# Key differences for both key halves of the first head group, with new planner settings

## The chip, the cores and the metric

The kernel runs on one core of one Trainium2 chip. The metric is device time in microseconds of one execution; a kernel's time is the median over its runs.

## The reference

Two transformer layers over 2048 rows of 512 columns. Each layer is an attention block with 32 heads of 16 columns and a gated feed-forward block of 1792 columns, both on a layer norm and both added back to x.

```python
def attention(x, wqkv, wo):            # x: (1, 2048, 512)
    q, k, v = split(x @ wqkv)          # 32 heads of 16 columns
    scores = einsum("bhqd,bhkd->bhqk", q, k) * 16 ** -0.5
    return merge(einsum("bhqk,bhkd->bhqd", softmax(scores), v)) @ wo

def ffn(x, w_gate, w_up, w_down):      # w_gate, w_up: (512, 1792)
    return (gelu(x @ w_gate) * (x @ w_up)) @ w_down

for layer in range(2):                 # the same weights in both
    x = x + attention(layernorm(x), A_wqkv, A_wo)
    x = x + ffn(layernorm(x), B_w_gate, B_w_up, B_w_down)
```

## The kernel before

**Units and tiles.** Heads go in groups of four (`NG` = 8), because four heads of 16 columns fit TensorE's four row groups of 32. The queries of a layer are cut into blocks (four of 512 in the first layer, three of 512 and two of 256 in the second, the last two handled in halves near the end). A unit `u` is one query block of one head group. A score tile is 128 queries of one head by 512 keys (one key block, `kb` 0 to 3); there are 4096 score tiles in all.

**Two passes over the scores.** The softmax needs a row maximum. In the first pass ("p1") TensorE makes a score tile with queries on the partitions (L1628) and VectorE reduces it to its row maximum in `PM` (L1643), one or two tiles per instruction. When a unit's maxima are all there, `fin_step` (L981 to L1012) joins the four key blocks' maxima in six small GpSimd operations, and a DVE transpose and four small DMAs (L1007, L1023) write the negated maximum into spare rows of the queries `QT`. In the second pass ("p2") TensorE makes the scores again, transposed, with the maximum already subtracted (L1510), ScalarE takes the exponential into `PT` (a view of `SCR`; L1487, one or two tiles per instruction), and TensorE multiplies by the values and a column of ones (L1533) into bank 7. `nrm` (L1031) divides.

**Folds.** VectorE has more to do in the first pass than ScalarE in the second at some times, so a pair of score tiles can be "folded". For key blocks a and b of one half of the keys, max(qa, qb) = qb + relu(qa - qb). GpSimd makes the key difference `KD` = KT[a] - KT[b] of the group once (`kd`, L1231 to L1243, the subtraction at L1240). TensorE multiplies the queries by it (L1460), ScalarE takes the Relu into `PT` (L1467), GpSimd writes a very negative maximum in place of tile a (L1470), and one custom VectorE instruction adds the Relu to tile b in PSUM and takes the maximum (L1638). Two VectorE tile reductions become one pass, and ScalarE gets one more. `f_list` holds the tiles that may be folded, in p1 order; `f_head` (L1404) drops those that p1 has passed, and `want_fold` (L1418) decides whether a fold is wanted. There are `NKD` = 2 buffers for differences. Before the change each unit has one pair of key blocks for its folds, and its buffer is `u % NKD`:

```python
pair = {u: (2, 3) if u == 0 else (0, 1) for u in range(NU)}
f_list = [h for h in p1_list if h[2] == pair[h[0]][0]]
```

**The order of the work.** The program is not looped on the chip. A planner at build time (the loop at L1668) steps through a model of the five engines and writes out each engine's instructions in order. It works through `p1_list`, keeps the second pass behind the first by a lag, and puts everything else (projections, layer norms, output projection, feed-forward pieces, differences) as chains with due times between them. For the first unit `p1_list` takes key block 0 of all queries first and key blocks 1 to 3 after that (L692). Every 32 score tiles (`STRETCH` = 16 pairs) the planner reads a new row of `PLAN`, 129 rows of 19 settings: how long an engine may wait for a joint start (`SPC`, `SPLIT`), lags from which evacuations change engine (`LAGT`) or the second pass gets more banks (`LAG`), whether pairs of banks may go to one exponential at two places (`P2B`), margins for folds (`FL`, `FX`), the size of projection pieces (`PIECE`, `GP`) and so on. PSUM evacuations go to VectorE (L766 `tensor_copy`) or ScalarE (L768) by `pick`. The same holds for the residual additions (L1064 on VectorE, L1069 with L1071 on ScalarE and GpSimd) and the gate products (L1195, or L1201 with L1203). Where TensorE would idle, the planner puts fill products on zeros (L1661).

In the head of the program GpSimd also clears the key buffers `KT` (the copies at L558), makes layer-norm scales (L581 to L585), normalises some rows (L592, which may also go to VectorE or ScalarE) and copies rows of x (L1293).

Of the kernel before, what the change touches and what calls it, by code (L numbers as in the profile page):

```python
# [310 lines left out]
def _build(nc, x_in, wqkv, wo, wg, wu, wd, out, layer_blocks=((512, 512, 512, 512), (512, 512, 512, 256, 256)),  # L311
# [16 lines left out]
    with es:  # L328
# [902 lines left out]
        def kd(u):  # L1231
# [4 lines left out]
            if pos["g"] >= f_end[u]:  # L1236
                return
# [653 lines left out]
```

## Time and profile before

| | |
|---|---|
| median of three runs | 2494.56 us (2493.24 to 2499.01) |
| the profiled execution's own time | 2493.29 us |
| its span | 2491.6 us |
| VectorE busy | 2417.7 us, 97% |
| ScalarE busy | 2339.2 us, 94% |
| TensorE busy | 2380.4 us, 96% |
| GpSimd busy | 1309.8 us, 53% |
| reductions at L1643 | 2595 instructions, mean 926 ns |
| exponentials at L1487 | 2484 instructions, mean 910 ns |
| folds at L1638 | 160 instructions, mean 686 ns |
| differences at L1240 | 74 instructions, mean 1153 ns |

The span runs from the first to the last instruction. Busy time is the union of an engine's instructions; neighbours on one engine may overlap a little in the records, so a mean duration is somewhat longer than the distance from one start to the next. In a group's line the number after the bar is busy time, then the mean of one, then the engine's idle time just before them with what ended it.

### The profile page before, as it was taken

What the parts mean: (1) busy time and instruction counts of PE and PEld (TensorE: products, weight loads), DVE (VectorE), ACT (ScalarE), POOL (GpSimd) and SP (SyncE); (2) the same over time, 40 slices, a digit from 0 to 9 for tenths busy, and PEclk for the clock granted to TensorE, in tenths of its full rate; (3) what the DMA queues carried; (4) which work ended last, traced back from release to release, by engine and by line L of the source; (5) the groups of instructions that cost most, each with busy time, mean ns of one, the idle gap of its engine ahead of it and who ended that gap; (6) DMA issues with size and microseconds to landing.
All of it is one profiled execution on the core that took longest, in us unless ns stands there. A gap on an engine that the chain in (4) does not pass through costs nothing.

```text
span 2491.6 us, 68681 instructions
## 1 busy us (share of the span) xinstructions
PE 2380.4 (96%) x29395; PEld 1138.3 (46%) x29648; DVE 2417.7 (97%) x3198; ACT 2339.2 (94%) x3189; POOL 1309.8 (53%) x2158
## 2 busy tenths in 40 slices
PE   7999999999999999999999999999999999999999
PEld 2444444444444444444433555554444444554456
DVE  9999999999999999999999999999999999999994
ACT  6999999999999999999965999999999999999996
POOL 5121138856788356877242211278617882269462
PEclk9999999999999999999999999999999999999999
DMA  3110000000000000000000000000000000000000
GB/s 94 48 57 6 6 2 9 2 4 4 4 4 2 2 7 4 4 10 2 17 7 12 5 4 4 4 4 2 2 13 6 2 3 11 4 3 4 9 5 10
DMA packets 27354, 25.09 MB, mean 10 GB/s; under 512 B 9513, under 2 KB 26025, under 8 KB 27049
## 3 DMA queue, kind: packets, MB, share of 16 engines
q1 hardware_dynamic: 27048, 20.69, 2.9%
q8 instruction: 232, 3.80, 0.6%
q14 instruction: 74, 0.60, 0.1%
HBM read 9.70 MB, written 2.10 MB: 5 GB/s over the span
## 4 chain that ended last, share of the span: by engine, by line
DVE 40%; PE 37%; ACT 22%; issue 1%; POOL 0%; DMA 0%; SPq 0%; ACTq 0%; POOLq 0%; DVEq 0%
DVE PM L1643 38%; ACT SCR L1487 20%; PE PS L1628 12%; PE PS L751 9%; PE PS L1533 8%; PE PS L1510 3%; PE PS L1661 3%; DVE SCR L1638 1%; ACT SCR L1127 1%; ACT SCR L1467 0%; PE PS L873 0%; PE PS L1460 0%; DVE HT L592 0%; ACT HT L768 0%; ACT AO L1201 0%
## 5 line engine op out<-in xcount | busy, mean ns | idle before, releaser
L1643 DVE TENSOR_REDUCE PM<-PS 128x1 f32<-128x512 f32 (+1 forms) x2595 | 2235.5, 926 | 30.8 <-PE PS L1510 9.3
L1487 ACT ACTIVATE SCR<-PS 128x1024 bf16<-128x1024 f32 (+1 forms) x2484 | 2029.4, 910 | 68.7 <-PE PS L1510 46.8
L1628 PE MATMUL PS<-KT,QT 32*128 32x512 bf16 x3936 | 1046.3, 384 | 54.4 <-DVE PM L1643 32.7
L1510 PE MATMUL PS<-QT,KT 32*128 32x512 bf16 (+2 forms) x4736 | 945.6, 354 | 6.0 <-ACT SCR L1487 5.0
L1533 PE MATMUL PS<-VP,SCR 128*128 128x51 bf16 (+1 forms) x16384 | 810.7, 187 | 11.8 <-ACT SCR L1487 6.8
L1533 PEld LDWEIGHTS PS<-VP,SCR 128*128 128x128 bf16 x16384 | 573.3, 96 | 497.6 <-issue 420.9
L1628 PEld LDWEIGHTS PS<-KT,QT 32*128 32x128 bf16 x3936 | 249.3, 91 | 533.3 <-DVE PM L1643 329.1
L1661 PE MATMUL PS<-WV,ZER 128*128 128x240 bf16 x1948 | 365.9, 266 | 4.8 <-ACT SCR L1487 3.4
L1051 POOL TENSOR_TENSOR RL<-ACCS,CM 128x16 f32<-128x16 f32 (+2 forms) x66 | 179.4, 2718 | 340.4 <-ACT ACCS L1045 340.0
L1510 PEld LDWEIGHTS PS<-QT,KT 32*128 32x128 bf16 x4736 | 239.0, 91 | 65.2 <-ACT SCR L1487 40.0
L996 POOL TENSOR_TENSOR PM<-PM 128x32 f32<-128x32 f32 (+2 forms) x74 | 18.0, 243 | 327.6 <-DVE PM L1643 320.8
L1661 PEld LDWEIGHTS PS<-WV,ZER 128*128 128x128 bf16 x1948 | 148.0, 96 | 61.0 <-issue 48.2
L1203 POOL TENSOR_TENSOR HT<-HT,AO 128x512 bf16<-128x512 bf16 x98 | 113.6, 1161 | 103.6 <-ACT AO L1201 103.1
L1240 POOL TENSOR_TENSOR KD<-KT 128x512 bf16<-128x512 bf16 x74 | 85.3, 1153 | 92.9 <-PE PS L1460 61.0
L751 PE MATMUL PS<-XNT,WU 128*128 128x512 bf16 (+2 forms) x498 | 123.6, 333 | 3.8 <-issue 2.5
L751 PE MATMUL PS<-XNT,WG 128*128 128x512 bf16 (+2 forms) x501 | 121.8, 333 | 5.2 <-issue 3.8
L751 PE MATMUL PS<-WD,HT 128*128 128x512 bf16 x384 | 121.2, 381 | 3.1 <-issue 1.3
L1131 POOL TENSOR_TENSOR HT<-HT,SCR 128x512 bf16<-128x512 bf16 (+1 forms) x98 | 106.1, 1083 | 4.7
L1125 POOL TENSOR_TENSOR SCR<-SCR,HT 128x512 bf16<-128x512 bf16 (+1 forms) x98 | 106.0, 1083 | 1.7
L1121 POOL TENSOR_TENSOR SCR<-HT 128x512 bf16<-128x512 bf16 (+1 forms) x98 | 95.8, 978 | 18.2 <-ACT HT L768 12.9
L1638 DVE CUSTOM_DVE_ANT_0 SCR<-PS,SCR 128x512 bf16<-128x512 f32 x160 | 102.8, 686 | 2.6 <-PE PS L1628 0.8
L1071 POOL TENSOR_TENSOR X<-X,AO 128x512 f32<-128x512 f32 x39 | 49.4, 1266 | 101.6 <-ACT AO L1069 101.2
(126 smaller groups left out, 1541.3 us busy)
## 6 DMA issues: line engine op xcount, KB each, us to landing
KT<-SG SPq DMA_DIRECT2D x64, 64.0 KB
QT<-SG SPq DMA_DIRECT2D x56, 64.0 KB
QT<-MT SPq DMA_DIRECT2D x224, 1.0 KB
out_dram<-AO SPq DMA_DIRECT2D x16, 128.0 KB, 1.7
WG<-in_B_w_gate_dram SPq DMA_DIRECT2D x4, 448.0 KB, 4.0
WU<-in_B_w_up_dram SPq DMA_DIRECT2D x4, 448.0 KB, 4.9
WD<-in_B_w_down_dram SPq DMA_DIRECT2D x4, 384.0 KB, 4.8
HT<-in_A_x_dram SPq DMA_DIRECT2D x2, 512.0 KB, 9.0
```

What stands on the lines that cost most here:

```text
L751: ins = e.matmul(out_ap, lhsT=l, rhs=r_, start=(i == 0), stop=(i == n - 1))
L1051: emit("pool", lambda e: e.tensor_tensor(RL[:, s, 0:4 * nq], lsum, CM1[:, 0:4 * nq], op=ALU.pow), r=[("ACCS", s), ("CM1",)], w=[("RL", s)] ...
L1125: emit("pool", lambda e: e.tensor_tensor(u, u, ht, op=ALU.mult), r=[ku, kh], w=[ku], dur=0.18 + n / 520.0)
L1131: emit("pool", lambda e: e.tensor_tensor(ht, ht, u, op=ALU.mult), r=[ku, kh], w=[kh], dur=0.18 + n / 520.0)
L1203: emit("pool", lambda e, ft=ft, o=o: e.tensor_tensor(HV[:, ft, :], HV[:, ft, :], AO[:, o, 0:n], op=ALU.mult), r=[("AO", o)] + ht_keys(ft, ...
L1487: emit("act", lambda e: e.activation(dst, src, ACTF.Exp, scale=DH ** -0.5), r=[BK[bk + i] for i in range(cnt)], w=[("PT", i) for i in slot ...
L1510: ins = e.matmul(bank(bk)[:, i * n:(i + 1) * n], lhsT=KT[32 * j:32 * j + 32, g, kt * 128:(kt + 1) * 128], rhs=QT[32 * j:32 * j + 32, s, 0: ...
L1533: ins = e.matmul(acc, lhsT=PT[:, slot, i * n + qt * 128:i * n + (qt + 1) * 128], rhs=AP(VP, (kt * H + 4 * g + j) * 17, [[NTT * H * 17, 128 ...
L1628: ins = e.matmul(bank(b), lhsT=QT[32 * j:32 * j + 32, s, qt * 128:(qt + 1) * 128], rhs=KT[32 * j:32 * j + 32, g, kb * 512:(kb + 1) * 512], ...
L1638: emit("dve", lambda e, i=i, b=b, sl=sl: e.tensor_tensor_reduce(PT[:, sl, :], bank(b), PT[:, sl, :], 1.0, -3.0e38, ALU.add, ALU.max, po[:, ...
L1643: emit("dve", lambda e: e.tensor_reduce(po, PS[:, bs[0]:bs[0] + cnt, :], axis=AX.X, op=ALU.max), r=bks, w=[("PM", sm) + h[1:] for h in hs] ...
L1661: return e.matmul(PS[:, b, NACC:512], lhsT=ZER[:, :], rhs=WV[:, 0, 0:512 - NACC], start=(b != 7), stop=(b != 7), skip_group_check=True)
```

## The change

`folds` replaces `pair`: a unit may fold in key half 0 (blocks 0 and 1), and units below `DP` = 1, so the first one alone, in half 1 (blocks 2 and 3) as well. Differences, their records and buffers are kept for a unit and a half instead of a unit: `f_seq` numbers them in p1 order, and the buffer is that number modulo `NKD`. In `fin_step` the maxima of neighbouring key blocks are now compared by stride instead of by first and second half, for all units, so that in each comparison the block whose maximum a fold replaces comes first. And 94 of the 129 rows of `PLAN` have new numbers: rows 0 to 5, 18 to 65, 73 to 79, and nearly all from 90 on.

```diff
 PLAN = [
-    (0.1, 0.0, 0.65, 0.42, 0.3, -0.05, 1, 1, 62, 84, 8, 80, 0.3, 2.0, 0, 2, 2, 2, 7),
+    (0.1, 0.0, 0.45, 0.12, 0.3, -0.05, 1, 1, 62, 84, 8, 60, 0.3, 1.5, 0, 2, 2, 2, 7),
...
-        pair = {u: (2, 3) if u == 0 else (0, 1) for u in range(NU)}
+        folds = {u: (0, 1) if u < DP else (0,) for u in range(NU)}
         p1_at = {h: i for i, h in enumerate(p1_list)}
-        f_list = [h for h in p1_list if h[2] == pair[h[0]][0]]
+        f_list = [h for h in p1_list if h[2] % 2 == 0 and h[2] // 2 in folds[h[0]]]
         f_end = {}
+        f_gs = []
+        half_p1 = {}
         for h in f_list:
-            f_end[h[0]] = max(f_end.get(h[0], -1), p1_at[h])
+            gi = (h[0], h[2] // 2)
+            if gi not in f_end:
+                f_gs.append(gi)
+                half_p1[gi] = p1_at[h] / 2.0
+            f_end[gi] = max(f_end.get(gi, -1), p1_at[h])
+        f_seq = {gi: i for i, gi in enumerate(f_gs)}
...
             if f["stage"] == 0:
-                lo, hi = pm[:, :, 0:8], pm[:, :, 8:16]
-                if pair[u][0] == 2:
-                    lo, hi = hi, lo
-                a0, a1 = lo[:, :, 0:4], lo[:, :, 4:8]
+                pv = pm.rearrange("p a (h l j) -> p a h l j", h=2, l=2)
+                lo, hi = pv[:, :, :, 0, :], pv[:, :, :, 1, :]
+                a0, a1 = lo[:, :, 0, :], lo[:, :, 1, :]
...
-        def kd(u):
+        def kd(gi):
+            u, hf = gi
             la, bi, t0, n, g = units[u]
-            ka, kb = pair[u]
+            ka, kb = 2 * hf, 2 * hf + 1
+            q = f_seq[gi]
             yield ("cond", lambda: (kt_rec.get((g, ka)) == la and kt_rec.get((g, kb)) == la
-                                    and (u < NKD or pos["g"] > f_end[u - NKD])))
+                                    and (q < NKD or pos["g"] > f_end[f_gs[q - NKD]])))
-            if pos["g"] >= f_end[u]:
+            if pos["g"] >= f_end[gi]:
                 return
-            s = u % NKD
+            s = q % NKD
...
-            for u in range(NU):
-                add(kd(u), first_p1[u] - FDUE)
+            for gi in sorted(f_gs):
+                add(kd(gi), (half_p1[gi] if gi[1] and gi[0] else first_p1[gi[0]]) - FDUE)
```

`f_head`, `f_opts` and `f_emit` look up the unit and half in the same way.

More of the change, by code (lines that the diff above doesn't have):

```diff
@@ L311, in _build @@
 def _build(nc, x_in, wqkv, wo, wg, wu, wd, out, layer_blocks=((512, 512, 512, 512), (512, 512, 512, 256, 256)),
-           n_ahead=6, n_pre=6, S1C=0.45, S2C=0.42, OV=0.3, PD=80, FDUE=20, LIM=-0.05, NT=1, AHD=2.0, DUEM=2, FDL2=0, OPD=12, URG=0.3, ft_tok=512, n_pt=8, n_qt=8, SPLIT=0.15, SPC=0.1, PVC=47, WARM=0.55, WARML=0.42, NPV=7, BOOST=0.0, LAG=62, LAGT=84, GP=2, SING=0, DUE=0, END=360, LAGE=10, FD=205, FDL=-10, QD=60, KD_=16, VD=20, FL=8, FMAX=6, NKD=2, FLOOK=2, FX=0.3, GF=0, FAST=1, TG=1, GS=2, P2B=1, PIECE=2, GL=60, GLE=20, HARD=-1e9, LNP=1, LNPT=12, PREO=1, SPL=2, OPL=1, BM=1, LAGB=60, PREO0=1, LNPT0=8, LNPT1=8):
+           n_ahead=6, n_pre=6, S1C=0.45, S2C=0.42, OV=0.3, PD=80, FDUE=20, LIM=-0.05, NT=1, AHD=2.0, DUEM=2, FDL2=0, OPD=12, URG=0.3, ft_tok=512, n_pt=8, n_qt=8, SPLIT=0.15, SPC=0.1, PVC=47, WARM=0.55, WARML=0.42, NPV=7, BOOST=0.0, LAG=62, LAGT=84, GP=2, SING=0, DUE=0, END=360, LAGE=10, FD=205, FDL=-10, QD=60, KD_=16, VD=20, FL=8, FMAX=6, NKD=2, FLOOK=2, FX=0.3, GF=0, FAST=1, TG=1, GS=2, P2B=1, PIECE=2, GL=60, GLE=20, HARD=-1e9, LNP=1, LNPT=12, PREO=1, SPL=2, OPL=1, BM=1, LAGB=60, PREO0=1, LNPT0=8, LNPT1=8, DP=1):
     S = x_in.shape[1]
@@ L1242, in kd @@
                  r=[("KT", g, ka), ("KT", g, kb)], w=[("KD", s)], dur=1.2)
-            kd_rec.add(u)
+            kd_rec.add(gi)
         hstat = {1}
@@ L1410, in f_head @@
             u = i[0]
-            if u not in kd_rec or u not in qt1_rec or (u >= n_ahead and u - n_ahead not in qp2_rec):
+            if (u, i[2] // 2) not in kd_rec or u not in qt1_rec or (u >= n_ahead and u - n_ahead not in qp2_rec):
                 return None
@@ L1431, in f_opts @@
             h = f_list[0]
+            kdk = ("KD", f_seq[(h[0], h[2] // 2)] % NKD)
             if gel["on"] is not None or h[3] % 2 or f_list[1:2] != [h[:3] + (h[3] + 1,)]:
@@ L1435, in f_opts @@
                     return []
-                tq = max(est([("QT", h[0] % n_qt), ("KD", h[0] % NKD)]), est(w=[("PT", so)]), now)
+                tq = max(est([("QT", h[0] % n_qt), kdk]), est(w=[("PT", so)]), now)
                 bs = (4,) if gel["on"] is not None else (6, 5) if wide else (6,)
@@ L1441, in f_opts @@
                 return []
-            tq = max(est([("QT", h[0] % n_qt), ("KD", h[0] % NKD)]), est(w=[("PT", sp), ("PT", sp + 1)]), now)
+            tq = max(est([("QT", h[0] % n_qt), kdk]), est(w=[("PT", sp), ("PT", sp + 1)]), now)
             return sorted((max(tq, est(w=[BK[b], BK[b + 1]])), b, 2, True) for b in ((3, 5) if wide else (4, 5))
@@ L1451, in f_emit @@
             s = u % n_qt
-            sd = u % NKD
+            sd = f_seq[(u, ka // 2)] % NKD
             sm = u % n_ahead
-            kb = pair[u][1]
+            kb = ka + 1
             def fn(e):
@@ L1567, in p1_turn @@
             for h in rest:
-                if h[2] == pair[h[0]][0]:
-                    f_end[h[0]] = p1_at[h]
+                if h[2] % 2 == 0 and h[2] // 2 in folds[h[0]]:
+                    f_end[(h[0], h[2] // 2)] = p1_at[h]
         def p1_skip():
```

182 rows, old and new, of the table PLAN are left out of this document.

## The prediction

> **What bounds the kernel now.** I read the page first: the busy shares, the row of slices and the chain that ended last.
>
> ```profile
> PE 2380.4 (96%) x29395; PEld 1138.3 (46%) x29648; DVE 2417.7 (97%) x3198; ACT 2339.2 (94%) x3189; POOL 1309.8 (53%) x2158
> ...
> DVE  9999999999999999999999999999999999999994
> ...
> DVE 40%; PE 37%; ACT 22%; issue 1%; POOL 0%; DMA 0%; SPq 0%; ACTq 0%; POOLq 0%; DVEq 0%
> ...
> DVE PM L1643 38%; ACT SCR L1487 20%; PE PS L1628 12%; PE PS L751 9%; PE PS L1533 8%; PE PS L1510 3%; PE PS L1661 3%; DVE SCR L1638 1%; ACT SCR L1127 1%; ACT SCR L1467 0%; PE PS L873 0%; PE PS L1460 0%; DVE HT L592 0%; ACT HT L768 0%; ACT AO L1201 0%
> ```
>
> VectorE (DVE) is busy 97% of the span and full in every slice but the last; its score reductions at L1643 alone are 38% of the chain, the exponentials of ScalarE (ACT) at L1487 are 20%. So the span is the DVE's work, plus its idle time, plus what is left when the last score has been reduced. When that is, the DVE's timeline says:
>
> ```profile
> 2436.50 2.41 DVE L1643 TENSOR_REDUCE PM<-PS 128x1 f32<-128x512 f32 x3
> ```
>
> The last reduction ends at 2436.50 + 2.41 = 2438.9 us. I then cut the span at places that are the same number of score tiles (128 queries by 512 keys; 4096 in all) done in both kernels. The columns are the length, then busy time and count of PE, weight loads, DVE, ACT and POOL.
>
> ```profile
> core 0: us, PE busy (x) PEld busy (x) DVE busy (x) ACT busy (x) POOL busy (x), PEclk, DMA share, GB/s
> 0.00:367.20 367.20, 344.74 (x4051) 162.75 (x4069) 360.57 (x543) 339.40 (x418) 96.79 (x181) 1.00 0.12 36
> 367.20:1192.60 825.40, 784.52 (x9696) 367.95 (x9798) 819.46 (x974) 803.76 (x1145) 584.12 (x964) 1.00 0.02 4
> 1192.60:1729.40 536.80, 523.92 (x6099) 244.20 (x6132) 520.39 (x749) 483.37 (x578) 203.93 (x353) 1.00 0.03 7
> 1729.40:2184.60 455.20, 433.63 (x5450) 206.09 (x5508) 453.09 (x563) 438.57 (x594) 244.56 (x357) 1.00 0.02 6
> 2184.60:2438.90 254.30, 245.14 (x3364) 123.66 (x3397) 246.86 (x323) 239.65 (x392) 172.39 (x288) 1.00 0.02 5
> 2438.90:2468.30 29.40, 28.37 (x477) 17.47 (x479) 6.82 (x17) 26.37 (x37) 7.44 (x17) 1.00 0.04 11
> 2468.30:2491.60 23.30, 20.08 (x269) 16.23 (x272) 10.48 (x39) 8.05 (x31) 0.55 (x1) 1.00 0.04 13
> ```
>
> DVE idle time, length less busy, is 6.6, 5.9, 16.4, 2.1 and 7.4 us in the first five rows, together 38.4. In the sixth (29.4 us) the DVE has next to nothing to do and ACT finishes its exponentials, in the seventh (23.3 us) the last feed-forward block runs. Thus 2438.9 + 29.4 + 23.3 = 2491.6 us of span. The profiled execution took 2493.29 us, 1.69 outside the span; the median of the three runs is 2494.56, 1.27 above it. I work out a difference and apply it to the median.
>
> **What the built order shows of the change.** The change makes key differences for keys 0 to 1023 and 1024 to 2047 of the first head group; a difference allows a "fold" (one DVE pass in place of two tile reductions, with a Relu on ACT). In the changed program's order the first group has 12 folds in its second half, as before, and none in its first half: scores of block 0 are scheduled before block 1's keys exist. The new difference is made and never used. So the named part is one POOL instruction, and the rest of the change is the order that the new settings give. Settings differ for score tiles 0-191, 576-2111, 2336-2559 and from 2880 on; from 2112 to 2880 both orders do the same work for each 128 tiles within 0.2 us. Counts over the whole program, before to after: DVE pair reductions 1181 to 1189, single ones 1414 to 1410, folds 160 to 154; ACT exponentials of 1024 columns 1612 to 1532, of 512 872 to 1032; fill products on PE 1948 to 1925; DMA issues 540 and 540. Nothing of the arithmetic goes away.
>
> **DVE work up to the last reduction.** The groups by shape:
>
> ```profile
> L1643 DVE TENSOR_REDUCE PM<-PS 128x2 f32<-128x1024 f32 x1181 | 1430.4, 1218 | 20.4 <-PE PS L1510 6.5 <-PE PS L1628 5.7
> ...
> L1643 DVE TENSOR_REDUCE PM<-PS 128x1 f32<-128x512 f32 x1414 | 946.2, 681 | 10.4 <-PE PS L1628 3.1 <-PE PS L1510 2.7 <-PE PS L1460 0.3
> ...
> L1638 DVE CUSTOM_DVE_ANT_0 SCR<-PS,SCR 128x512 bf16<-128x512 f32 x160 | 102.8, 686 | 2.6 <-PE PS L1628 0.8 <-PE PS L1460 0.6 <-PE PS L1510 0.2
> ...
> L1064 DVE TENSOR_TENSOR X<-PS,X 128x512 f32<-128x512 f32 x9 | 6.2, 684 | 2.8 <-PE PS L751 2.6
> ...
> L592 DVE TENSOR_SCALAR HT<-HT 128x512 bf16<-128x512 bf16 x8 | 3.9, 551 | 0.0
> ...
> L766 DVE CAST HT<-PS 128x256 bf16<-128x256 f32 x2 | 0.8, 415 | 0.0
> ...
> L766 DVE COPY XNT<-PS 128x512 bf16<-128x512 bf16 x11 | 4.5, 413 | 1.5 <-PE PS L873 1.5
> ```
>
> Two merged rows of the chain give the pace behind these durations:
>
> ```profile
> 558.72 37.17 DVE PM L1643 x44
> ...
> 1601.29 29.56 ACT SCR L1487 x32
> ```
>
> 44 reductions in 37.17 us are 0.845 each, where the mean by the two forms is 0.925: neighbours overlap by 0.08. So a pair costs 1.14, a single 0.60, a fold 0.61. Eight pairs more are +9.1, four singles less -2.4, six folds less -3.7: +3.0. The copies that the planner gives to the DVE instead of ACT: one more of L766 at 256 columns into HT and one into SG (0.33 each), two at 128 into SG (an estimate of 0.2 each from the step between the 256 and 512 forms), two more transposed tiles (0.33 each): +1.7. Two additions of L1064 fewer (0.60 each) and one normalisation of L592 fewer (0.41): -1.6. The 256-column products of L1195 fall from 14 to 10, but up to the last reduction they are 9 and 9. Sum **+3.1 us**, bounds +2 (if the copies are covered by idle time) and +4.
>
> ACT takes two copies of L1069 and four of L1201 more, hands about as many others to the DVE, and gets the split exponentials:
>
> ```profile
> L1487 ACT ACTIVATE SCR<-PS 128x1024 bf16<-128x1024 f32 x1612 | 1583.7, 1070 | 60.2 <-PE PS L1510 43.1 <-PE PS L1628 0.4
> ...
> L1487 ACT ACTIVATE SCR<-PS 128x512 bf16<-128x512 f32 x872 | 522.7, 615 | 8.5 <-PE PS L1510 3.7
> ```
>
> By the means a pair split in two costs 2 x 0.615 - 1.070 = 0.16 us; by the chain row, 32 exponentials in 29.56 us or 0.92 each, the overlap of 0.15 makes it about 0.01. Eighty splits are 0.8 to 12.8 us; the row of neighbours in a run is nearer, so I take about 1. It lies beside DVE work: ACT idles (709.5 - 678.21) = 31.3 us between 1729.4 and 2438.9, as the second row here shows.
>
> ```profile
> 1400.00:1729.40 329.40, 321.92 (x4435) 165.14 (x4452) 321.27 (x420) 328.68 (x376) 135.81 (x219) 1.00 0.02 4
> 1729.40:2438.90 709.50, 678.76 (x8812) 329.76 (x8903) 699.95 (x884) 678.21 (x985) 416.95 (x644) 1.00 0.02 6
> ```
>
> If that cover were gone, the first row shows the price: with ACT full (0.7 us idle of 329.4) the DVE idles 8.1 us, 2.5%.
>
> **The head.** POOL is the engine that gets the added difference (1.15 us), and its fills of KT move: one now stands before the last row block's layer-norm scales, and the DVE's normalisations come as three and four with five and seven tiles around them. How the two engines meet is seen in the first 50 us, DVE rows, then POOL rows:
>
> ```profile
> 8.54 3.97 DVE L592 TENSOR_SCALAR HT<-SCR,HT 128x512 bf16<-128x512 bf16 x2 [0.35 <-POOL HT L603]
> ...
> 24.80 1.37 DVE L592 TENSOR_SCALAR HT<-HT 128x512 bf16<-128x512 bf16 x4
> ...
> 27.83 2.54 DVE L592 TENSOR_SCALAR HT<-HT 128x512 bf16<-128x512 bf16 x4
> ...
> 30.29 15.99 DVE L1643 TENSOR_REDUCE PM<-PS 128x1 f32<-128x512 f32 x19
> ```
>
> ```profile
> 8.58 3.78 POOL L558 COPY KT<-HT 128x2048 bf16<-128x2048 bf16 x2
> ...
> 26.49 1.89 POOL L558 COPY KT<-HT 128x2048 bf16<-128x2048 bf16 x1
> ...
> 28.95 2.45 POOL L1293 CAST X<-HT 128x512 f32<-128x512 bf16 x4
> ...
> 36.15 1.15 POOL L1240 TENSOR_TENSOR KD<-KT 128x512 bf16<-128x512 bf16 x1 [2.91 <-DMA KT<-SG]
> ```
>
> Two DVE normalisations last 3.97 us while POOL's two copies run from 8.58 to 12.36; four others take 1.37 in one place and 2.54 in the other, where POOL's copy of 1.89 (26.49 to 28.38) overlaps their start. The added difference itself follows the one at 36.15, beside reductions (19 in 15.99 us, the 0.84 pace): reductions read PSUM and are not held, so it costs 0 there; what it moves back on POOL is the next group's difference, first needed some 30 tiles later, and the KT fill behind that. The buffers, now given out by halves, add a wait as well: the second group's difference takes the first half's buffer, so it waits until score tile 16; nothing on the DVE waits for it before the folds of the second group. In the new order both groups of normalisations may meet a copy: 0 to 3.8 us against 1.2 now, that is -1.2 to +2.6. PE also has longer stretches without a score tile there (five of over 1.2 us in the first 640 tiles, two before), which can starve the DVE by some tenths each. I take **+1.5**, range -1.2 to +4, since the DVE idle time of the first row (6.6 us) shows that this part is not padded.
> The Trainium skill, page "SBUF — State Buffer", section "SBUF: two separate sides", says that VectorE in a two-port mode and GpSimd share one port pair as an exclusive lock held for a whole instruction, so that the loser blocks fully. By that rule the head could lose the full overlap of both groups, 2.6 us rather than my 1.5; the 3.97 us row agrees with the rule, and the sum would move by 1.1.
>
> **Idle time of the DVE in the changed stretches.** It has 5.9 us in the second row and 9.5 in the fourth and fifth. It comes where PE has long work between two score tiles. These stretches can be counted in both orders, at the paces of the chain in which PE ends last:
>
> ```profile
> 2450.03 1.02 PE PS L751 x4
> ...
> 2451.06 0.34 PE PS L1510 x8
> ```
>
> With 0.25 us for a 512-column product at most, 0.04 for a value product (eight in about 0.31) and a quarter of a pass for row-group tiles, stretches of over 1.0 us from tile 2944 on are 16 before and 10 after; from 640 to 2048 they are five and six. So 9.5 us might fall to 9.5 x 10/16 = 5.9 (-3.6), or not at all. I take **-1.5**, nearer to nothing, as the many shorter waits stay.
>
> **The tail.** Between the last score tile and the last exponential the new order has 46 exponential tiles where there were 54, 4 gate products of 256 columns for 18, and 411 matmuls for 492. That stretch is a chain of PE and ACT:
>
> ```profile
> by line: PE PS L1510 27.9%; PE PS L751 25.7%; PE PS L1533 20.1%; ACT SCR L1487 15.4%; ACT L1148 4.0%; PE PS L1661 2.9%; issue 1.5%; ACT HT L1182 1.0%; ACT SCR L1127 0.9%; ACT SQ L1148 0.6%; ACT ACCS L1045 0.4%
> ```
>
> In proportion to matmuls 29.4 x 411/492 = 24.6: **-4.8 us**. Bounds: four pairs at 0.92 are -3.7; with 14 gate products at 0.13 more, -5.5. After the last exponential both programs have the same 288 matmuls, and 23.3 us stay. The DVE has done more by then, which is the +3.1 above.
>
> **Other moves.** The six POOL steps per group that end the maxima read another layout of the same 32 numbers, and two additions and four products more go to POOL, 53% busy: nothing, under a backlog of about a hundred tiles. No DMA moves in number.
>
> **Sum.** +3.1 + 1.5 - 1.5 - 4.8 = -1.7 us; 2494.56 - 1.7 gives 2492.9, taken as **2493**. That is within 0.2% (5 us, 2489.6 to 2499.5), about what a measurement of this kernel can tell from no change: its three runs alone spread over 5.8 us.
>
> **Rivals.** *The new order removes waits.* The DVE's idle time in the changed stretches halves, (5.9 + 9.5)/2 = 7.7, and the head costs nothing: 3.1 - 7.7 - 4.8 = -9.4, 2485. For it: fewer long PE stretches late, and no added work to speak of. Against: the idle time is already under 1.5% and lies in many short waits; 36%.
> *ACT becomes the bound after the middle.* The 512-column exponentials cluster from tile 2944 on (381 before, 522 after). If splitting costs the 0.16 of the separate means, 70 net splits are 11 us, and with the waits of PE for banks ACT's 31.3 us of idle time go; from then the DVE idles at 2.5% as between 1400 and 1729.4, 709.5 x 0.025 = 17.7 for 9.5: +8.2. Then 3.1 + 1.5 + 8.2 - 4.8 = +8.0, 2502.6. It decides once ACT's idle time there is under some 5 us. Against it: the pace of 0.92. 25%.
> *The change is inert,* the shorter tail and longer reduction part just cancelling, 2494 to 2495: within the forecast's 39%.
>
> The range reaches from near the first rival to the second, 2484 to 2502. Chances: faster 0.36, same 0.39, slower 0.25.
>
> **What would show it.** In the profile after: 154 custom DVE passes; the last reduction at about 2438.9 + 3.1 + 1.5 - 1.5 = 2442; 24 to 26 us from there to the last exponential and 23 after it. Wrong is the head if the DVE's idle time by tile 640 differs by over 4 us from 6.6; wrong is the work term if the DVE's busy time leaves 2417.7 by more than 4; the first rival shows as less DVE idle time in both changed stretches, the second as ACT idle under 5 us late.

## The result, and the profile after

The kernel after takes 2496.58 us (median, 2496.41 to 2501.1), the kernel before 2493.23 in the same comparison (13 runs of each): a ratio of 1.0014, 95% interval 1.0007 to 1.0020, or +3.35 us. The forecast was -1.6. The profiled execution has a span of 2494.6 us, 3.0 longer than before. From its page, the busy line, the DVE's slices and the two rows of the chain that ended last:

```profile
PE 2387.8 (96%) x29366; PEld 1143.7 (46%) x29625; DVE 2421.0 (97%) x3189; ACT 2337.4 (94%) x3267; POOL 1316.8 (53%) x2164
...
DVE  9999999999999999999999999999999999999994
...
PE 44%; DVE 37%; ACT 17%; issue 1%; POOL 0%; POOLq 0%; DVEq 0%; ACTq 0%
DVE PM L1652 35%; ACT SCR L1496 16%; PE PS L1637 15%; PE PS L1542 10%; PE PS L758 10%; PE PS L1519 4%; PE PS L1670 3%; DVE SCR L1647 0%; PE PS L1469 0%; ACT SCR L1476 0%; DVE HT L575 0%; ACT SCR L1133 0%; PE PS L880 0%; DVE HT L592 0%; ACT HT L775 0%
```

Most lines of the program have moved down by five to nine: the reduction is L1652 (was L1643), the exponential L1496 (L1487), the first-pass score tile L1637 (L1628), the second-pass one L1519 (L1510), the value product L1542 (L1533). The DVE still sets the pace, but PE's share of the chain has grown from 37% to 44%, and that of the DVE and ACT has fallen; first-pass score tiles alone are 15% of it, for 12%. The DVE's last reduction, and then the stretches cut at the same numbers of score tiles as in the prediction (length, then busy time and count of PE, weight loads, DVE, ACT, POOL):

```profile
2441.10 5.50 DVE L1652 TENSOR_REDUCE PM<-PS 128x2 f32<-128x1024 f32 x6
```

```profile
core 0: us, PE busy (x) PEld busy (x) DVE busy (x) ACT busy (x) POOL busy (x), PEclk, DMA share, GB/s
0.00:369.00 369.00, 345.77 (x4061) 164.07 (x4078) 361.86 (x541) 339.12 (x417) 98.92 (x186) 1.00 0.12 36
369.00:1194.60 825.60, 789.39 (x9638) 368.83 (x9741) 818.43 (x980) 797.86 (x1153) 583.94 (x963) 1.00 0.02 5
1194.60:1733.00 538.40, 525.54 (x6151) 246.91 (x6182) 520.60 (x748) 485.90 (x581) 206.27 (x355) 1.00 0.03 6
1733.00:2197.30 464.30, 444.24 (x5576) 213.17 (x5642) 461.01 (x556) 449.35 (x682) 249.14 (x362) 1.00 0.02 6
2197.30:2446.60 249.30, 238.93 (x3292) 119.92 (x3319) 243.39 (x317) 235.15 (x379) 173.12 (x287) 1.00 0.02 5
2446.60:2471.30 24.70, 23.84 (x395) 14.54 (x400) 5.17 (x13) 21.95 (x30) 4.84 (x13) 1.00 0.04 13
2471.30:2494.60 23.30, 20.08 (x269) 16.22 (x272) 10.52 (x39) 8.09 (x32) 0.55 (x1) 1.00 0.04 13
```

The last reduction ends at 2446.6, 7.7 us later than before; from there to the last exponential there are 24.7 us in place of 29.4, and 23.3 after it as before. So +7.7 - 4.7 = +3.0. The 7.7 divide by the first five rows into DVE busy time, 2405.3 against 2400.4 (+4.9), and DVE idle time, 7.1, 7.2, 17.8, 3.3 and 5.9 us against 6.6, 5.9, 16.4, 2.1 and 7.4: 41.3 against 38.5, +2.8 (38.4 in the prediction is the sum of rounded terms). (The fourth stretch is longer and the fifth shorter because after runs some 20 second-pass tiles further ahead there.) The groups by shape, DVE and ACT:

```profile
L1652 DVE TENSOR_REDUCE PM<-PS 128x2 f32<-128x1024 f32 x1189 | 1439.5, 1217 | 22.3 <-PE PS L1637 7.4 <-PE PS L1519 6.4
L1652 DVE TENSOR_REDUCE PM<-PS 128x1 f32<-128x512 f32 x1410 | 943.3, 681 | 10.5 <-PE PS L1637 3.2 <-PE PS L1519 3.1 <-PE PS L1469 0.2
L1647 DVE CUSTOM_DVE_ANT_0 SCR<-PS,SCR 128x512 bf16<-128x512 f32 x154 | 99.1, 685 | 2.6 <-PE PS L1637 1.0 <-PE PS L1469 0.6
```

```profile
L1496 ACT ACTIVATE SCR<-PS 128x1024 bf16<-128x1024 f32 x1532 | 1501.4, 1073 | 58.4 <-PE PS L1519 42.7 <-DVE PM L1652 0.5 <-PE PS L1637 0.4
L1496 ACT ACTIVATE SCR<-PS 128x512 bf16<-128x512 f32 x1032 | 604.2, 619 | 15.0 <-PE PS L1519 9.1
```

The counts are those that the prediction read from the order. The head, DVE rows and then POOL rows:

```profile
25.29 2.29 DVE L592 TENSOR_SCALAR HT<-HT 128x512 bf16<-128x512 bf16 x3
...
31.56 2.48 DVE L592 TENSOR_SCALAR HT<-HT 128x512 bf16<-128x512 bf16 x4
```

```profile
24.90 1.89 POOL L558 COPY KT<-HT 128x2048 bf16<-128x2048 bf16 x1
...
30.45 1.89 POOL L558 COPY KT<-HT 128x2048 bf16<-128x2048 bf16 x1
32.28 1.28 POOL L1301 CAST X<-HT 128x512 f32<-128x512 bf16 x2
```

Both groups of normalisations now start under a running copy, where before one of them did.

### The profile page after: what moved, and what is told of

Same layout as the page of the kernel before. It is cut to its first block, busy times and chain, and to the rows that moved or that the text cites. A ratio compares the mean times of both kernels' runs of the same rounds, so it can differ in the third digit from the quotient of the medians.

```text
span 2494.6 us, 68685 instructions
## 1 busy us (share of the span) xinstructions
PE 2387.8 (96%) x29366; PEld 1143.7 (46%) x29625; DVE 2421.0 (97%) x3189; ACT 2337.4 (94%) x3267; POOL 1316.8 (53%) x2164
## 4 chain that ended last, share of the span: by engine, by line
PE 44%; DVE 37%; ACT 17%; issue 1%; POOL 0%; POOLq 0%; DVEq 0%; ACTq 0%
DVE PM L1652 35%; ACT SCR L1496 16%; PE PS L1637 15%; PE PS L1542 10%; PE PS L758 10%; PE PS L1519 4%; PE PS L1670 3%; DVE SCR L1647 0%; PE PS L1469 0%; ACT SCR L1476 0%; DVE HT L575 0%; ACT SCR L1133 0%; PE PS L880 0%; DVE HT L592 0%; ACT HT L775 0%
## 5 line engine op out<-in xcount | busy, mean ns | idle before, releaser
L1652 DVE TENSOR_REDUCE PM<-PS 128x1 f32<-128x512 f32 (+1 forms) x2599 | 2242.8, 926 | 32.9 <-PE PS L1637 10.6
L1496 ACT ACTIVATE SCR<-PS 128x1024 bf16<-128x1024 f32 (+1 forms) x2564 | 2031.8, 890 | 73.4 <-PE PS L1519 51.8
L1637 PE MATMUL PS<-KT,QT 32*128 32x512 bf16 x3942 | 1047.4, 385 | 56.3 <-DVE PM L1652 32.3
L1519 PE MATMUL PS<-QT,KT 32*128 32x512 bf16 (+2 forms) x4736 | 960.0, 354 | 4.4 <-ACT SCR L1496 2.7
L1542 PE MATMUL PS<-VP,SCR 128*128 128x51 bf16 (+1 forms) x16384 | 822.9, 187 | 11.0 <-ACT SCR L1496 6.3
L1542 PEld LDWEIGHTS PS<-VP,SCR 128*128 128x128 bf16 x16384 | 578.3, 96 | 513.6 <-issue 435.0
L1637 PEld LDWEIGHTS PS<-KT,QT 32*128 32x128 bf16 x3942 | 250.0, 91 | 520.6 <-DVE PM L1652 303.8
L1519 PEld LDWEIGHTS PS<-QT,KT 32*128 32x128 bf16 x4736 | 242.6, 91 | 66.9 <-ACT SCR L1496 40.5
L1209 POOL TENSOR_TENSOR HT<-HT,AO 128x512 bf16<-128x512 bf16 (+1 forms) x102 | 116.3, 1142 | 113.6 <-ACT AO L1207 112.2
L1476 ACT ACTIVATE SCR<-PS 128x1024 bf16<-128x1024 f32 (+1 forms) x79 | 81.3, 1029 | 20.6 <-PE PS L1469 18.8
```

The costliest lines, as they stand in the source:

```text
L1209: emit("pool", lambda e, ft=ft, o=o: e.tensor_tensor(HV[:, ft, :], HV[:, ft, :], AO[:, o, 0:n], op=ALU.mult), r=[("AO", o)] + ht_keys(ft, ...
L1496: emit("act", lambda e: e.activation(dst, src, ACTF.Exp, scale=DH ** -0.5), r=[BK[bk + i] for i in range(cnt)], w=[("PT", i) for i in slot ...
L1519: ins = e.matmul(bank(bk)[:, i * n:(i + 1) * n], lhsT=KT[32 * j:32 * j + 32, g, kt * 128:(kt + 1) * 128], rhs=QT[32 * j:32 * j + 32, s, 0: ...
L1542: ins = e.matmul(acc, lhsT=PT[:, slot, i * n + qt * 128:i * n + (qt + 1) * 128], rhs=AP(VP, (kt * H + 4 * g + j) * 17, [[NTT * H * 17, 128 ...
L1637: ins = e.matmul(bank(b), lhsT=QT[32 * j:32 * j + 32, s, qt * 128:(qt + 1) * 128], rhs=KT[32 * j:32 * j + 32, g, kb * 512:(kb + 1) * 512], ...
L1652: emit("dve", lambda e: e.tensor_reduce(po, PS[:, bs[0]:bs[0] + cnt, :], axis=AX.X, op=ALU.max), r=bks, w=[("PM", sm) + h[1:] for h in hs] ...
```

## The experiments

Every time below is a median, compared with the kernel before on the same chip (2493.05 to 2493.22 us in the four comparisons); differences are to that. The 95% intervals of the ratio are up to 0.0013 (3 us) wide to each side. By them the two kernels with tiles moved ahead, the one with groups parted, the code alone, the whole groups moved ahead and after without its new difference are slower than before, and before with all three edits is faster; all other runs can't be told from before by their interval alone. Differences of some tenths of a us rest on the medians.

**Code and settings apart.** The first kernel is before with after's `PLAN`. Its order on PE, DVE, ACT and the DMA queues is after's; it lacks the new difference and keeps the old layout of the maxima. The second is after with before's `PLAN`.

```diff
 # first: the kernel before
-PLAN = [...before's 129 rows...]
+PLAN = [...after's 129 rows...]
```

> The kernel before with the new settings alone (no differences by halves, old layout of the maxima). Its order on TensorE, VectorE, ScalarE and the DMA queue is instruction by instruction that of the changed kernel; GpSimd has one difference less in the head and the old layout of the six maximum steps. Theory A (the settings carry the loss): as slow as the changed kernel, +2.5 to +3.4 us over before, and not more than 1 us faster than the changed kernel. Rival B (the halves of the differences cost it, through GpSimd): within 0.5 us of the kernel before.

2496.23 us, +3.04: the settings carry the loss, and the code on top of them 0.3.

> The changed code with the old settings. Theory A: the added difference has an order of its own only in the first units, so 0 to +2 us over before. Rival B: about +3 us. Rival C (the difference disturbs the order, and the new settings were needed to mend that): clearly worse than both kernels, +5 us or more, with the loss before score tile 512, where its order leaves that of the kernel before; behind tile 640 it is the order of before.

2504.82 us, +11.6 (ratio 1.0039, 1.0027 to 1.0051). The difference shifts the built order, and with the old settings the shifted order is a bad one. Its trace shows where most of it goes: 8.0 us of DVE idle time between score tiles 384 and 512, where before has 0.7. DVE rows, then a PE row:

```profile
240.21 0.69 DVE L773 CAST SG<-PS 128x512 bf16<-128x512 f32 x1 [3.39 <-PE PS L758]
241.71 0.69 DVE L773 CAST SG<-PS 128x512 bf16<-128x512 f32 x1 [0.81 <-PE PS L758]
243.44 1.82 DVE L1652 TENSOR_REDUCE PM<-PS 128x2 f32<-128x1024 f32 x2 [1.04 <-PE PS L1637]
```

```profile
239.14 1.68 PE L758 MATMUL PS<-XNT,WK 128*128 128x512 bf16 x7
```

The key projection of the next head group is late, no score tile can be made, and the DVE waits 3.39 + 0.81 + 1.04 us. So the new settings take up what the added difference does to the order, and bring it back to 3 us behind before. Whether other settings would do so better was not run.

**Which settings.** Three kernels are before with some of after's rows: 90 and up, 18 to 65, 0 to 5 (score tiles 0 to 191, not 0 to 95 as the third expectation has it). Rows 73 to 79 were not run alone.

> The kernel before with the new settings from row 90 (score tile 2880) on alone. By the traces of the two kernels this part loses 7.7 - 2.4 = 5.3 us up to the last reduction and wins 4.7 us behind it: theory A: +0.6 us over before, with the last reduction 5 us later and 24 to 25 us from there to the last exponential. Rival (parts of the order do not add up, the late loss depends on what came before): outside 0 to +1.5 us.

> The kernel before with the new settings in rows 18 to 65 (score tiles 576 to 2111) alone. By the two traces the changed kernel is 1.8 us late at tile 640 and 2.5 us at tile 2176, so theory A gives +0.7 us over before, all of it as VectorE idle time (6 to 7.2 us between tiles 640 and 2048). Rival (parts do not add up): outside 0 to +1.5 us.

> The kernel before with the new settings of score tiles 0 to 95 alone (the first six lines of the list). Theory A (the head loses a part of its own: the DVE's normalisations held by two KT copies on POOL, 1.2 us more than before, and 0.6 us more idle time by tile 128): +1.1 to +1.8 us on the kernel before, 2494.3 to 2495.0, with the normalisations again as two groups of over 2.2 us. By the sum of parts, 3.35 - 0.35 - 1.08 - 0.82 = 1.1 is what is left for these lines. Rival B (the loss hangs on all lines together): 0 within 0.3 us, 2493.2, or over 3 us.

2494.01 (+0.82), 2494.27 (+1.08) and 2494.73 us (+1.61). With the 0.3 of the code they add up to 3.8 for 3.35 measured: no single stretch is at fault, and about half is the head's. The +0.82 of the late rows is a net: the last reduction ends at 2444.1 us, 5.2 later than before, and what follows it is 4.7 shorter. In the head run the normalisations are held as in after:

```profile
25.34 2.28 DVE L592 TENSOR_SCALAR HT<-HT 128x512 bf16<-128x512 bf16 x3
...
31.60 2.47 DVE L592 TENSOR_SCALAR HT<-HT 128x512 bf16<-128x512 bf16 x4
```

**The hold in the head.** From here on kernels keep their instructions and change the order of a few. The recorded operations are laid out again with the moved ones in their new place, and all waits are worked out anew from what each reads and writes.

```diff
+EARLY = [((30, 38), 15)]     # (note) POOL's operations 30 and 38, two KT copies, go behind its operation 15
...
+        sch = sch.again(AHEAD, EARLY)
         sch.plan()
```

> The kernel after with the two KT copies that stood at 24.90 and 30.45 us on POOL moved ahead to where the first two copies end (12.3 us; POOL then waits 4.57 us for the DVE's statistics); every other instruction keeps its place on its engine. Theory A (these copies hold the DVE's normalisations): the groups of three and four, 2.29 and 2.48 us, go to about 1.0 and 1.4, so -1.2 to -2.4 us by tile 128 and -1.2 to -2.4 at the end, 2494.2 to 2495.4. Rival B (something else is slow there, such as the POOL's casts at L1301 or the DVE's own reads): the groups stay over 2 us and the time stays at 2496.6 within 0.4. Rival C: the hold goes, but the gain is lost in later waits: head -1.2 or more, end 0.

2495.22 us, +2.10 where after has +3.35. DVE rows, then the POOL row of what are now four copies in one:

```profile
25.26 1.05 DVE L630 TENSOR_SCALAR HT<-HT 128x512 bf16<-128x512 bf16 x3
...
30.92 1.37 DVE L630 TENSOR_SCALAR HT<-HT 128x512 bf16<-128x512 bf16 x4
```

```profile
8.50 7.51 POOL L596 COPY KT<-HT 128x2048 bf16<-128x2048 bf16 x4
```

4.77 us of normalisations have become 2.42, so they had been held for 2.35: 1.24 in the group of three, under the copy at 24.90, and 1.11 in the group of four. Theory A holds for the first. In the second the copy at 30.45 ran for only 0.78 us more when the group started at 31.56, and the casts of L1301 followed it at 32.28. They move away from the normalisations in this run too, so it does not part the copy from the casts there. 1.25 of the 2.35 arrive at the end, and 1.0 is DVE idle time by tile 128 (5.4 us for 4.4): the DVE's waits for first-pass tiles up to there are 1.6 us in place of 0.8.

**Score tiles moved ahead on PE.** The next two take the waits one by one.

```diff
+AHEAD = [(1662, 2, 1664), (1946, 1, 1947), (2156, 4, 2160), ...   # (note) first, count, last:
+        # PE's operations first to first + count - 1 go behind its operation last
```

> The kernel after with 61 score tiles or pairs, with the second-pass tiles beside them, moved on PE ahead of one to four value, projection or fill products that stood directly before them. They are those at whose reduction the trace of after shows the DVE idle for over 0.06 us between 300 and 2430 us, and whose PSUM bank had been free in time; their waits sum to 10.7 of 30.9 us. All other work and every other order stays. Theory A (the DVE's waits are PE's order: a score tile queued behind other products while its bank is free): most of the 10.7 us goes, the DVE's idle time to the last reduction falls from 41.3 to 31 to 36, and the time falls by 5 to 10 us, 2486.5 to 2491.5. Rival B (PE, 96% busy, is full there, and the waits come back behind it): idle time of 40 or more, time 2495.5 to 2497.

> The same edit made on the kernel before: 54 score tiles or pairs with waits of 10.1 of 28.7 us between 300 and 2430 us. Theory A: the DVE's idle time to the last reduction falls from 38.5 to 28 to 34 us and the time by 5 to 10 us, 2483 to 2488; the kernel after with the same edit stays 1 to 3 us behind it. Rival B: 2492.2 to 2493.5, idle time 37 or more.

2507.82 us (+14.7, 11.3 behind after) and 2503.70 (+10.6): neither theory. The edit did something that I had not seen. A score tile uses 32 of PE's 128 rows, and where first- and second-pass tiles stand next to each other in the order, PE works on several of them at once. I call such a run of row-group tiles, between two full products, a group. My edit put a product between a first-pass tile and the second-pass tiles beside it, and so made 37 more groups in after and 39 more in before (changes between row-group tiles and full products 5640 to 5714, 5578 to 5656). If these are all of the loss, it is 0.31 and 0.27 us for each parted group. Counted in the same way, the change under study itself goes from 5578 to 5640: 31 groups more. That goes with its 80 fewer exponentials of two tiles, for which second-pass tiles are sent one at a time. The runs with the late rows alone and the first layer's rows alone have 10 and 16 groups more in their traces.

**Whole groups, parted groups, joined groups.** Three kernels test that. The first moves a group only as a whole; the second parts 39 groups where the DVE was not waiting; the third joins 40 pairs of neighbours.

> The kernel after, as in the run with 61 tiles moved ahead, but a score tile now takes along all row-group tiles that follow it, so that none is parted from the second-pass tiles that run beside it. 27 such groups have all their banks free early enough; their waits are 4.2 of 32.8 us. Changes of PE between row-group tiles and full products: 5612 where after has 5640 and the run that parted the groups 5714. Theory A (waits are PE's order): -2 to -4.2 us, 2492.4 to 2494.6. Theory S (what counts is the changes between the two kinds, 0.15 us each by the 11.2 us that 74 more cost): 28 x 0.15 = -4.2, the same. Rival B (PE is full and the waits come back): 2496 to 2497.

> The kernel before with 39 groups parted: one value product is moved from ahead of a first-pass score tile to between it and the second-pass tiles beside it, at places where the trace of before shows that tile's reduction starting over 0.3 us after its matmul and the DVE without a wait. Changes between row-group tiles and full products 5656, as in the run of before with tiles moved ahead (2503.7), against 5578 in before. Theory S (a change costs PE's 0.14 us wherever it stands): +9 to +11 us, 2502 to 2504. Theory C (it costs only where the DVE or ACT is already waiting for PE; elsewhere the backlog of scores hides it): 0 to +3, by the rate of the two runs with some of the new settings, 1.9 us for 52 changes or 0.037 each; 2493.2 to 2496.1. Rival: below 2493.

> The kernel before with 40 pairs of neighbouring row-group batches joined: one to three value or fill products that stood between them on PE now follow the second one, at places where its banks had been free in time. Changes 5498 against 5578. Theory S: 80 x 0.14 = -11 us, 2482. Theory C: -3 to 0, 2490 to 2493.2, by 0.037 each. Rival D (the joined tiles collide with the engines that drain the banks): over 2493.2.

2495.45 us for the first (+2.40, so 0.95 better than after, for the 2 to 4.2 expected). The second is at 2500.91, +7.86 (ratio 1.0037, 1.0023 to 1.0050), 0.20 us a group: near theory S, far from C, so the backlog of scores does not hide it. The third is at 2491.64, -1.41 (0.9993, 0.9984 to 1.0001), 0.035 us a pair, as theory C has it. Parting a group costs nearly six times what joining two gives. (Joining also moves the second group ahead of the products between them, so the two effects are not apart here.) PE rows of one place, before and with the group parted:

```profile
482.56 0.69 PE L1533 MATMUL PS<-VP,SCR 128*128 128x34 bf16 x12
483.18 0.38 PE L1628 MATMUL PS<-KT,QT 32*128 32x512 bf16 x1
483.18 0.39 PE L1510 MATMUL PS<-QT,KT 32*128 32x512 bf16 x2
483.50 0.28 PE L1533 MATMUL PS<-VP,SCR 128*128 128x34 bf16 x4
```

```profile
483.22 0.38 PE L1577 MATMUL PS<-VP,SCR 128*128 128x34 bf16 x8
483.53 0.39 PE L1672 MATMUL PS<-KT,QT 32*128 32x512 bf16 x1
483.85 0.28 PE L1577 MATMUL PS<-VP,SCR 128*128 128x34 bf16 x4
484.06 0.39 PE L1554 MATMUL PS<-QT,KT 32*128 32x512 bf16 x2
484.38 0.28 PE L1577 MATMUL PS<-VP,SCR 128*128 128x34 bf16 x4
```

In before the first-pass tile and two second-pass tiles start together at 483.18, and from 12 value products to the next ones PE takes 483.50 - 482.56 = 0.94 us. Parted, the same work goes one after the other, 484.38 - 483.22 = 1.16. The 0.22 more is close to the 0.20 a place of the whole run. From a group's start to the next full product these rows have 0.32 us each time, for the group of three tiles (483.18 to 483.50), the one tile (483.53 to 483.85) and the group of two (484.06 to 484.38): parted, the 0.32 is paid twice.

The Trainium skill, page "TensorEngine Tiling (Array Packing)", section "Key Properties", says that a change of tiling mode drains TensorE, and that different tiles work in parallel. The trace agrees with the second, since a group's tiles start together. How much of the 0.32 us a drain would be, no row here shows.

**The waits in the records.** The row of the DVE's reductions, in before, in the two runs that parted groups of it (where the DVE waited, and where not), in before with 40 pairs of groups joined, then in after with the copies early and in the mended kernel of the next part, each with busy time, mean and idle time ahead:

```profile
L1643 DVE TENSOR_REDUCE PM<-PS 128x1 f32<-128x512 f32 (+1 forms) x2595 | 2235.5, 926 | 30.8 <-PE PS L1510 9.3 <-PE PS L1628 8.7 <-PE PS L1460 0.3
```

```profile
L1690 DVE TENSOR_REDUCE PM<-PS 128x1 f32<-128x512 f32 (+1 forms) x2595 | 2236.9, 924 | 38.1 <-PE PS L1557 14.5 <-PE PS L1675 10.3 <-PE PS L1507 0.9
```

```profile
L1687 DVE TENSOR_REDUCE PM<-PS 128x1 f32<-128x512 f32 (+1 forms) x2595 | 2236.2, 924 | 37.0 <-PE PS L1554 14.5 <-PE PS L1672 9.7 <-PE PS L1504 0.3
```

```profile
L1687 DVE TENSOR_REDUCE PM<-PS 128x1 f32<-128x512 f32 (+1 forms) x2595 | 2233.6, 924 | 30.8 <-PE PS L1554 9.1 <-PE PS L1672 8.5 <-PE PS L1504 0.3
```

```profile
L1690 DVE TENSOR_REDUCE PM<-PS 128x1 f32<-128x512 f32 (+1 forms) x2599 | 2242.7, 925 | 34.0 <-PE PS L1675 11.4 <-PE PS L1557 9.7 <-PE PS L1507 0.2
```

```profile
L1695 DVE TENSOR_REDUCE PM<-PS 128x1 f32<-128x512 f32 (+1 forms) x2599 | 2241.7, 925 | 33.4 <-PE PS L1680 10.5 <-PE PS L1562 10.3 <-PE PS L1512 0.2
```

Parted groups turn into idle time of the DVE: 7.3 and 6.2 us more of it, most behind second-pass tiles (9.3 to 14.5). Joined pairs don't show the other way round: in before they leave the idle time at 30.8 and take 1.9 us off the busy time.

**Mended.** One kernel is after with the two copies early and 31 pairs of groups joined, so that it has before's 5578 changes. One is before with all that helped. One is after without the new difference.

```diff
 # the last one
-        folds = {u: (0, 1) if u < DP else (0,) for u in range(NU)}
+        folds = {u: (1,) if u < DP else (0,) for u in range(NU)}
```

> The kernel after with the two late KT copies early (2495.2 alone) and with 31 pairs of neighbouring groups joined, so that it changes between row-group tiles and full products 5578 times, as before does, in place of 5640. Theory G (the 31 more groups are what is left of the loss, 1.9 us): 2493.3 within 0.4. Theory P (a pair joined gives 0.035 us, whatever it was before): 2494.1 within 0.3. Rival (the groups have nothing to do with it): 2495.2.

> The kernel before with three edits of the order: the first two late KT copies moved into POOL's wait at 12.3 us, 18 whole groups moved ahead on PE where the DVE waited, and 36 pairs of neighbouring groups joined; changes between row-group tiles and full products 5488 for 5578. By the rates of the runs with one edit each (-1.2 for the hold in before's head, -0.04 a group moved ahead, -0.035 a pair joined) -1.2 - 0.7 - 1.3 = -3.2, 2489.9. Rival: they don't add up, and it stays at the 2491.6 of the joined pairs alone.

> The kernel after with the difference for the first half of the first head group's keys left out, and nothing else changed: one subtraction of 1.15 us less on POOL at 35.11 us. Theory (it is never used, and beside score reductions it holds nothing): 2496.6 within 0.3. Rival (it makes the head late, or holds the DVE): -0.35 to -1.2, 2495.4 to 2496.2; the kernel before with the new settings, which lacks it too but has the old layout of the maximum steps, was at 2496.2.

After mended is at 2493.56 us, +0.34 on before (ratio 1.0001, 0.9992 to 1.0010): the two kernels are level, as theory G had it. This does not show that the 31 groups were the rest of the loss. Joining pairs makes before faster too, where no group had been added, and by its rate there (0.035) 31 pairs are 1.1 of the 1.76 us that they gave here (0.057 each). Nor are the pairs that could be joined the groups that the settings had added. The stretch up to the last reduction in before, after, after without the new difference and after mended (columns as above):

```profile
0.00:2438.90 2438.90, 2331.95 (x28652) 1104.65 (x28898) 2400.37 (x3145) 2304.74 (x3123) 1301.78 (x2140) 1.00 0.04 10
0.00:2446.60 2446.60, 2343.86 (x28702) 1112.90 (x28953) 2405.29 (x3139) 2307.39 (x3208) 1311.40 (x2151) 1.00 0.04 10
0.00:2446.40 2446.40, 2379.05 (x28953) 1112.56 (x28953) 2404.98 (x3139) 2307.45 (x3208) 1313.64 (x2150) 1.00 0.04 10
0.00:2443.60 2443.60, 2375.55 (x28953) 1111.72 (x28953) 2401.70 (x3139) 2306.76 (x3208) 1314.75 (x2151) 1.00 0.04 10
```

After mended still idles 2443.60 - 2401.70 = 41.9 us on the DVE, after 41.3 and before 38.5. From score tile 640 on it is 33.8, for 34.2 and 31.9. So most of the waits that the change added are still there. The kernel is level because its busy time is 3.6 us under after's, 2.35 of them the hold in the head, and because it keeps after's shorter tail: against before, busy time +1.3, idle time +3.4, what follows the last reduction -4.7. On PE the joined pairs did free time: the last two rows have the same 28953 matmul records (the first two lack some), and PE's busy time falls from 2379.1 to 2375.6 us, 0.11 a pair. (Moving the copies alone left PE's busy time of after as it was.)

In the reductions' row the joined pairs took 1.0 us of busy time (2242.7 to 2241.7) and 0.6 of idle time (34.0 to 33.4). Why busy time falls was not tested; one reading is this: neighbouring reductions overlap by 0.08 us in the records, so a wait shorter than that shows as less overlap and longer busy time.

Before with all three is at 2490.78 us (2490.55 to 2490.92), -2.44, ratio 0.9987 (0.9978 to 0.9996): the fastest of all, and ahead of both kernels, if by 0.1%. The edits don't quite add up (-3.2 expected). After with its copies early and pairs joined stays 2.8 us behind it; it has 90 changes more, and no group of it was moved ahead as a whole.

After without the new difference is at 2496.29, 0.3 better than after and level with the run of the settings alone. So the named part costs 0.3 us at most with these settings and gives nothing; its trace doesn't show where the 0.3 lies.

## Why the prediction was wrong

The forecast was a shorter time, and after is 3.35 us longer. The last reduction was to end at about 2442 and ends at 2446.6, 4.6 us late; the 154 folds, the tail and the work up to it came nearly as forecast. The term that failed is the DVE's idle time.

**Right: what the change is.** The new difference is made and never used, as the order showed; the folds are 154, and the rest is the order that the settings give.

**Nearly right: the DVE's work, +3.1, and the head, +1.5.** Busy time to the last reduction rose by 4.9. Of that 1.2 are the hold of the normalisations that the head's term contains (2.35 us of the 4.77 for seven; in before 1.37 + 2.54 for eight, of which 1.17 beyond twice the free 1.37). The counts are those forecast and at the prediction's prices 3.1; the 0.6 that is left is a slightly longer pace of the reductions. The head lost 1.9 us by tile 128 and 1.6 at the end in the run with its rows alone. The head's hold was 1.2 us more than before, not the 2.6 that a loss of both copies' full length would give. When the DVE came to its two groups, the copies had 26.79 - 25.29 = 1.50 and 32.34 - 31.56 = 0.78 us to run; that is 2.28 in sum for 2.35 held, but group by group it was 1.24 and 1.11. The rule of an exclusive lock that the prediction took from the Trainium skill's page "SBUF — State Buffer", section "SBUF: two separate sides", agrees with the sum, if the DVE loses only what is left of a copy when it arrives; the split it leaves open. In before, too, the copy that the prediction saw had only 28.38 - 27.83 = 0.55 us to run where 1.17 was held, and a cast followed it on POOL; that casts hold the DVE as well was not tested. The batch-norm statistics beside the moved copies kept their pace: 0.66 us each with and without a copy, and the first reduction started at 23.02 us, and 23.06 in after.

**Right: the tail, -4.8.** It measured -4.7: 24.7 us to the last exponential, where the 411 of 492 matmuls had given 24.6.

**Wrong: idle time of the DVE in the changed stretches, -1.5.** Outside the first stretch idle time rose by 2.3, and with the reductions' pace that is +2.9, 4.4 us off: this gives the answer its sign. The late stretch itself did fall by the 1.5 forecast (7.4 to 5.9), but the three ahead of it rose by 1.2, 1.4 and 1.2. The step counted PE stretches of over 1.0 us between two score tiles, with estimated paces: 16 before and 10 after from tile 2944 on, five and six from 640 to 2048. In the traces, gaps of over 1.0 us between one first-pass matmul and the next are 39 and 37 in the first of these parts and 29 and 20 in the second, and in the second the DVE's idle time rose all the same. So this count does not tell the idle time. What grew were the many short waits: outside the first stretch the DVE's waits of 0.06 to 0.5 us sum to 22.7 us before and 25.8 after, while those over 0.5 us fell from 5.9 to 5.2.

What made the short waits grow is not shown in full. The prediction put a price on the 80 split exponentials on ACT alone (about 1 us beside DVE work), and none on PE, where there are 31 groups more. By the joined pairs in before (0.035 us each) these are 1.1 us, by the parted groups (0.20) 6.2, so they are large enough to matter; the first layer's rows alone have 16 groups more, 1.5 us more idle time and +1.08 us in the time. But no run took out the added groups themselves, and joining 31 other pairs left the idle time nearly where it was (42.4 us with the copies early, 41.9 with the pairs joined too). Shown is that the settings carry 3.0 of the 3.35 us, that the head's rows alone bring 1.6, and that without the hold after is 1.25 faster (before has a smaller hold of its own). For the rest the groups are the likeliest cause, and it stays open.

**The rivals.** The first (order removes waits, 2485) and the second (ACT the bound, 2502.6) did not happen: between 1733.0 and 2446.6 ACT idles 713.6 - 449.35 - 235.15 = 29.1 us (31.3 before), far from the 5 us at which it would decide, and the DVE's idle time fell in one stretch only. The median of before is now 1.3 us lower than the one of three runs that the forecast started from; that does not touch the difference.

## What to carry to other kernels

Where tiles that use part of TensorE's rows run side by side, count the groups of them in the built order before moving single tiles. Here 37 to 39 parted groups cost 8 to 11 us, 0.20 us each even where the engine behind had a backlog, and moving 27 groups as a whole to where they were wanted won 1 us. A change that shifts a planned order must be priced by the whole order that results, on every engine that a split touches: the named part of this one cost 0.3 us with the new settings and 11.6 with the old ones. And check a rule that counts long stretches against the trace of the kernel before, which already has the waits. In a kernel's head, clear buffers on GpSimd while VectorE does something that isn't held; here that won 1.25 us.

## What the runs showed of the hardware

- A group of one first-pass and two second-pass tiles takes 0.32 us on PE from its start to the next full product, and a single tile takes the same; with value products put inside, the same work takes 0.22 us more. Over 39 places it was 0.20 each on average where the DVE had a backlog and 0.27 where it waited.
- A GpSimd copy from SBUF to SBUF (1.89 us) held three bf16 normalisations of VectorE for 1.24 us; a copy and the casts behind it held four for 1.11. Batch-norm statistics took 0.66 us each beside such copies and without them, and reductions from PSUM kept their pace of 0.84 beside them (19 in 15.99 us, in before).
